# Loads ahead of transposes, weights cast by loads, linear term last: a one-core attention and maxout kernel

## The chip, the cores and the metric

One of the eight cores of a Trainium2 chip runs the whole program. The metric is the device time of one execution in microseconds (us). TensorE multiplies, VectorE and ScalarE move and change data, GpSimd does small sums and issues the loads, SyncE issues the stores and the transposing transfers. The profile calls them PE, DVE, ACT, POOL and SP; PEld is the loading of the weights into TensorE.

## What is computed

```python
B, N, m, C = 4, 12544, 32, 128          # x: (B, N, C), inducing: (m, C)
h = mab(I, x)                           # 32 inducing points attend to the N rows of a batch
y = mab(x, h)                           # every row attends to its batch's 32 rows of h
# mab(q, kv): a = softmax(q @ kv.T / sqrt(C)); return a @ kv
g = max(y @ w1, y @ w2)                 # w1, w2: (128, 1024)
out = g @ w_out                         # w_out: (1024, 128); out: (50176, 128), f32
```

## The kernel before, in words

Since max(p, q) = p + relu(q - p), the output of a row is y @ (w1 @ w_out) + relu(y @ (w2 - w1)) @ w_out, and since y is a mean over the 32 rows of h, two products are made once for each batch: `hwd` = h @ (w2 - w1), 32 x 1024 (`small_hwd`), and `m1` = h @ (w1 @ w_out), 32 x 128 (`small_m1`). For every row TensorE then needs its 32 exponentials `e2` (`stage`), their product with `hwd`, a relu, and the product of that with `w_out`. The denominator `rp` (`dens`) is multiplied in at the very end (`evict_group`).

A batch has 98 chunks of 128 rows. Its tokens come in seven tiles of 14 chunks (`load_x`, a load that casts f32 to f16, issued by GpSimd, L165). Phase one makes h: the tile is transposed into `xT`, `p1_scores` (L239) multiplies it with the inducing points, ScalarE takes the exponential `et` (L248), `p1_accum` (L282) sums et times x. For batch 0 TensorE makes the transposes (`p1_transpose`) and also sums et with a matrix of ones (L269). For batches 1 to 3 the transposes are transfers that SyncE issues, two to a tile (`transpose_x_dma`, L171), the sum of et is made by GpSimd (L290, L295, `small_fold` L300 and L301), and phase one of a batch is spread over the main loop of the batch before it.

The main loop works on blocks of four quarters of the columns. `phase` (L730) makes four matmuls side by side, 32 rows each, whose results four relus of 128 x 512 take out of PSUM, on ScalarE (L746) or VectorE (L749), whichever the planner holds free earlier. `final_one` then makes the eight products with `w_out` for each of four chunks (L575, 32 matmuls of 128 columns), into a PSUM bank that already holds the linear term e2.T @ m1. The first blocks of batch 0 (`full`; the "ramp") are narrow, one or two chunks to a quarter; there the linear term comes from `m1bd`, a block-diagonal copy of m1, by four matmuls ahead of the 32 (L563); in the other blocks it comes from `phase`. `evict_group` scales four chunks (L601, L604, L611) and SyncE stores them (L626), from six buffers.

The order on each engine is written by a planner at build time. Class `Clock` holds an estimate of when each engine and PSUM bank is free, and the main loop picks a phase or a final matmul by it. Side work is tied to a count: `at(n, f, ...)` puts f on a list that `side_work` starts once n chunks of output have been evicted. Since engines work in order, what is written behind a waiting instruction on the same engine waits too.

Weights: three loads (L202 to L204) bring w2, w1 and w_out as f32. `weights_1` subtracts (VectorE, L372). Behind the first two phases and the staging of block 1 stand `weights_2` (a cast of w_out by ScalarE, L376; eight f32 transposes of w1 by TensorE, L383, and two casts of them, L387), `weights_3` (w1 @ w_out, L394, L402) and `small_m1(0)` (L357, L360, and four copies to `m1bd` by ScalarE, L364). Only then come the final matmuls of the first group.

Of the kernel before, what the change touches and what calls it, by code (L numbers as in the profile page):

```python
# [9 lines left out]
F16 = mybir.dt.float16  # L10
# [6 lines left out]
INF = 1e9  # L17
# [91 lines left out]
def kernel(  # L109
# [17 lines left out]
    P1 = 14  # L127
    WARM = 12

# [55 lines left out]
    wof = relup.tile([128, 2, J], F32, name="wof", tag="relu1")  # L185
    woutf = wof[:, 0, :].rearrange("p (jb c) -> p jb c", c=C)
# [7 lines left out]
    with tc.manual_schedule(engines={ET.PE, ET.DVE, ET.Activation, ET.Pool, ET.SP}):  # L194
# [7 lines left out]
        nc.gpsimd.dma_start(out=w2f, in_=moe_w2)  # L202
        nc.gpsimd.dma_start(out=w1f, in_=moe_w1)
        nc.gpsimd.dma_start(out=woutf, in_=moe_w_out.rearrange("(jb j) c -> j jb c", j=128))  # L204
# [47 lines left out]
        def p1_accum(b, i):  # L252
# [3 lines left out]
            if b == 0:  # L256
                last = i == len(parts[0]) - 1
                ck.wait(ready, "p1")
                for j in range(n):
# [6 lines left out]
                    )  # L266
                for j in range(0, n, 4):
# [5 lines left out]
                        start=(i == 0 and j == 0),  # L273
# [80 lines left out]
        def small_m1(b):  # L354
# [6 lines left out]
            if b in (0, 1, 2, 3):  # L361
                for q in range(4):
                    r = slice(32 * q, 32 * (q + 1))
                    nc.scalar.copy(out=m1bds[b % 2][r, q, :], in_=ps[r, 0:128])  # L364
                ck.on_act(end, 0.8)
# [5 lines left out]
        def weights_1():  # L371
            nc.vector.tensor_sub(w21, w2f, w1f)  # L372
            ck.on_dve(0.0, 1.2)

        def weights_2():
            nc.scalar.copy(out=woutp, in_=woutf)  # L376
            ck.on_act(0.0, 1.0)
            for g in range(2):
                bi, ps = bank([128, 512])
                ck.wait(ck.bank[bi], "w")  # L380
                for j in range(4):
                    jb = 4 * g + j
                    nc.tensor.transpose(  # L383
                        ps[:, 128 * j : 128 * (j + 1)], w1f[:, 128 * jb : 128 * (jb + 1)], identity32
                    )
                end = ck.run(0.9)
                nc.scalar.copy(out=w1T[:, 4 * g : 4 * g + 4, :], in_=ps)  # L387
                ck.bank[bi] = w_of["w1T"] = ck.on_act(end, 0.48)

        def weights_3():  # L390
# [12 lines left out]
            ck.bank[bi] = ck.on_dve(end, 0.2)  # L403
# [86 lines left out]


# [61 lines left out]
        def final_one():  # L553
# [4 lines left out]
            if g.ps is None:  # L558
# [3 lines left out]
                for s, (q, t) in enumerate(g.chunks):  # L562
                    nc.tensor.matmul(  # L563
                        out=g.ps[:, 128 * s : 128 * (s + 1)],
                        lhsT=g.blk.e2[:, 128 * t : 128 * (t + 1)],
                        rhs=m1bds[g.blk.quarters[q].b % 2][:, q, :],
                        start=(s == 0),
# [307 lines left out]
```

## Time and profile before

| what | value |
|---|---|
| median of 3 runs | 359.9 us (358.38 to 362.74) |
| the profiled execution, its own time | 362.34 us |
| its span, from the first to the last instruction | 360.6 us |
| mean granted TensorE clock | 0.965 |
| PE, PEld, DVE, ACT, POOL busy | 339.7, 260.9, 291.1, 277.1, 43.2 us |
| DMA | 50.60 MB moved, mean 140 GB/s |

The timeline of slices gives the busy tenths of each engine in 40 equal parts, PEclk being the clock that TensorE was granted in tenths of full speed. In tables by window, each engine has its busy time and, in brackets, its number of instructions; then come the clock, the share of the 16 DMA engines and the rate. In timelines a row has its start, its duration, the engine and line, and in square brackets the idle time before it and what ended that. SPq and POOLq are issues of transfers, not their landing.

### The profile page before, as it was taken

The page shows a single profiled execution, that of the slowest core. Times are in us where ns is not written, and L with a number is a line of the kernel's source. Part 1 is how long each engine was busy: PE and PEld are TensorE (multiplying, and loading weights), DVE is VectorE, ACT ScalarE, POOL GpSimd, SP SyncE. Part 2 cuts the span into 40 slices and gives each one's busy share as a digit, 9 for nine tenths or more (in the row PEclk, how much of TensorE's full clock was granted, in tenths as well). Part 3 has the DMA queues.
Part 4 walks back from the last instruction along what each step waited for, and adds up shares of the span by engine and source line. Part 5 has one row for each costly group of instructions (what it writes and reads, how often), then busy time and mean ns, then how long its engine had stood idle before and what let it go on. Part 6 is the DMA issues. An engine that isn't in the chain of part 4 may idle for free.

```text
span 360.6 us, 13062 instructions
## 1 busy us (share of the span) xinstructions
PE 339.7 (94%) x5655; PEld 260.9 (72%) x5655; DVE 291.1 (81%) x529; ACT 277.1 (77%) x541; POOL 43.2 (12%) x69
## 2 busy tenths in 40 slices
PE   7867989999999994999999998999999999999996
PEld 3754867677778573778777776778777777777786
DVE  1344789998997993799989998688899989999972
ACT  2547789988885893788798987788889888889850
POOL 6320011115000021013200011213000000000000
PEclk9985899999999998899999999899999999999999
DMA  7999559684957799283992699883132223222223
GB/s 134 210 293 214 123 151 146 109 174 105 234 156 162 139 133 204 66 165 115 177 228 91 129 204 146 197 159 116 62 119 88 79 86 121 89 90 89 89 89 133
DMA packets 58089, 50.60 MB, mean 140 GB/s; under 512 B 41104, under 2 KB 41776, under 8 KB 58032
## 3 DMA queue, kind: packets, MB, share of 16 engines
q1 hardware_dynamic: 53424, 35.35, 39.9%
q0 software_dynamic: 4608, 14.42, 21.5%
q8 instruction: 44, 0.72, 0.8%
q14 instruction: 13, 0.11, 0.1%
HBM read 27.28 MB, written 25.69 MB: 147 GB/s over the span
## 4 chain that ended last, share of the span: by engine, by line
PE 78%; DMA 12%; ACT 4%; DVE 3%; issue 1%; POOL 1%; SPq 1%; POOLq 0%; ACTq 0%; DVEq 0%
PE ps L575 50%; PE ps L730 18%; DMA xT<-xn 9%; DMA xn<-in_x_dram 3%; PE ps L435 2%; ACT relu L746 2%; PE ps L239 2%; PE ps L282 2%; DVE relu L749 2%; PE ps L563 1%; PE ps L476 1%; PE ps L320 1%; PE ps L223 0%; ACT xT L230 0%; POOL xn L165 0%
## 5 line engine op out<-in xcount | busy, mean ns | idle before, releaser
L746 ACT ACTIVATE relu<-ps 128x512 f16<-128x512 f32 x449 | 238.5, 601 | 42.0 <-PE ps L730 37.0
L749 DVE TENSOR_SCALAR relu<-ps 128x512 f16<-128x512 f32 x335 | 215.6, 682 | 32.9 <-PE ps L730 28.8
L575 PE MATMUL ps<-woutp,relu 128*128 128x128 f16 x3136 | 226.9, 222 | 0.1
L575 PEld LDWEIGHTS <-relu 128*128 128x128 f16 x3136 | 181.0, 99 | 39.5 <-issue 29.7
L730 PE MATMUL ps<-e,hwd 32*128 32x512 f16 (+2 forms) x928 | 91.6, 359 | 0.4 <-DVE hwd L346 0.4
L601 DVE TENSOR_TENSOR o<-ps,rp 128x512 f32<-128x512 f32 x88 | 60.1, 683 | 9.1 <-PE ps L575 7.0
L730 PEld LDWEIGHTS <-hwd 32*128 32x128 f16 x928 | 25.7, 94 | 23.0 <-issue 2.6
L730 PE MATMUL ps<-m,e 32*128 32x128 f16 x336 | 33.7, 219 | 0.1
L295 POOL TENSOR_TENSOR eacc<-eacc,et 128x448 f32<-128x448 f32 x18 | 18.6, 1035 | 94.0 <-ACT et L248 94.0
L248 ACT ACTIVATE et<-ps 128x448 f16<-128x448 f32 (+2 forms) x29 | 15.6, 539 | 13.0 <-PE ps L239 10.1
L239 PE MATMUL ps<-inducingT,xT 128*128 128x32 f16 x392 | 16.0, 177 | 9.0 <-DMA xT<-xn 8.1
L730 PEld LDWEIGHTS <-e 32*128 32x128 f16 x336 | 19.0, 93 | 2.8 <-issue 0.3
L239 PEld LDWEIGHTS <-xT 128*128 128x128 f16 x392 | 13.3, 96 | 10.4 <-DMA xT<-xn 8.5
L447 ACT ACTIVATE e<-ps 128x512 f16<-128x512 f32 (+2 forms) x31 | 16.4, 529 | 2.3 <-PE ps L435 2.3
L165 POOL DMA_DIRECT2D xn<-in_x_dram x29 | 15.7, 548 | 9.8 <-DMA xn<-in_x_dram 4.9
L227 DVE COPY xT<-ps 128x1024 f16<-128x1024 f16 (+2 forms) x8 | 5.1, 633 | 11.7 <-PE ps L223 11.7
L290 POOL CAST eacc<-et 128x448 f32<-128x448 f16 x3 | 1.7, 558 | 101.0 <-ACT et L248 101.0
L435 PE MATMUL ps<-xT,hT 128*32 128x512 f16 (+2 forms) x124 | 11.4, 359 | 1.3 <-DVE hT L327 1.1
L230 ACT COPY xT<-ps 128x768 f16<-128x768 f16 (+2 forms) x8 | 5.6, 705 | 8.5 <-PE ps L223 8.5
L282 PE MATMUL ps<-et,xn 128*128 128x32 f16 x294 | 10.7, 178 | 0.0
L282 PEld LDWEIGHTS <-xn 128*128 128x128 f16 x294 | 9.9, 97 | 0.1
L223 PE MATMUL ps<-identity,xn 128*128 128x128 f16 x98 | 6.8, 219 | 1.9 <-DMA xn<-in_x_dram 1.9
(61 smaller groups left out, 109.6 us busy)
## 6 DMA issues: line engine op xcount, KB each, us to landing
out_dram<-o SPq DMA_DIRECT2D x96, 256.0 KB, 2.3
xn<-in_x_dram POOLq DMA_DIRECT2D x27, 448.0 KB, 11.8
wf<-in_moe_w_dram POOLq DMA_DIRECT2D x2, 512.0 KB, 14.8
xT<-xn SPq DMA_TRANSPOSE x42, 3.8
wof<-in_moe_w_out_dram POOLq DMA_DIRECT2D x1, 512.0 KB, 14.1
out_dram<-o SPq DMA_DIRECT2D x4, 128.0 KB, 2.4
xn<-in_x_dram POOLq DMA_DIRECT2D x1, 256.0 KB, 13.5
xn<-in_x_dram POOLq DMA_DIRECT2D x1, 192.0 KB, 13.9
```

Of the source, the lines that this page charges most:

```text
L165: nc.gpsimd.dma_start(out=xn_at[b, i][:, 0:n, :], in_=xr[b, :, k0 : k0 + n, :])
L239: nc.tensor.matmul(out=ps[:, j * M : (j + 1) * M], lhsT=xT_tiles[b % 2][:, k0 + j, :], rhs=inducingT, start=True, stop=True,)
L248: nc.scalar.activation(out=et[:, 0:n, :], in_=ps[:, 0 : n * M], func=AF.Exp, scale=scale)
L282: nc.tensor.matmul(out=ps[:, 0:M], lhsT=xn[:, j, :], rhs=et[:, j, :], start=(j == 0), stop=(j == n - 1))
L295: nc.gpsimd.tensor_add(out=acc, in0=acc, in1=et)
L435: nc.tensor.matmul(out=ps[32 * q : 32 * (q + 1), 128 * t : 128 * (t + n)], lhsT=hq, rhs=xT[:, c : c + n, :], start=True, stop=True, tile_p ...
L447: nc.scalar.activation(out=blk.e2[:, 0 : 128 * wd], in_=ps[:, 0 : 128 * wd], func=AF.Exp, scale=scale)
L575: nc.tensor.matmul(out=g.ps[:, 128 * c : 128 * (c + 1)], lhsT=g.blk.relu[q][:, 128 * (jb * w4 + t) : 128 * (jb * w4 + t + 1)], rhs=woutp[: ...
L601: nc.vector.tensor_mul(osb[:, 0:n, :], g.ps[:, 0 : n * C].rearrange("p (s c) -> p s c", s=n), rp)
L730: nc.tensor.matmul(**seq[i])
L746: nc.scalar.activation(out=dst, in_=src, func=AF.Relu)
L749: nc.vector.tensor_scalar(out=dst, in0=src, scalar1=0.0, scalar2=None, op0=ALU.max)
```

## The change

All of it is order, types and places; the mathematics stays.

1. Loads of batches 2 and 3: `load_x(b, i)` at base - 34 + 3 i instead of base - 26 + 6 i, base being the count at which the batch before is done (98, 196). The last is then due at base - 16, before the first transpose and before phase one of that batch. The transposes are due at base - 12 + 3.4 j instead of base - 16 + 4 j.
2. Batch 1: transposes at 9 + 2.3 j instead of 1 + 3 j; scores of tile i at 17 + 5.2 i instead of 10 + 6.3 i.
3. Weights: w2 and w1 come in halves of 512 columns (four loads), w1 comes a second time as f16 (`w1h`), and w_out is cast by its load into `woutp`. `weights_1` subtracts in two halves.
4. `weights_2` has eight f16 transposes of `w1h`, one result copied by VectorE and one by ScalarE, and stands right behind `small_hwd(0)`, ahead of the first phases. `small_m1(0)` becomes side work behind the start of the main loop.
5. In full blocks the four linear matmuls come behind the 32 final ones. The copies to `m1bd` are split between VectorE and ScalarE, in all batches.
6. Batch 0's first five sums of et are made by VectorE, with one f32 matmul of ones at the end; 14 matmuls on the `warm` tile (`fill`) stand between phase one of batch 0 and its first staging.
7. The condition on `tp` near the end is written in another way; with MARGIN = 0 it says the same.

GpSimd at the end of batch 1's phase one, before. The eacc rows are its sums of et for batch 1 (1023) and batch 2 (2982); xn rows are loads of batch 2.

```order
L300 TENSOR_TENSOR eacc_1023<-eacc_1023 128x224
L301 TENSOR_TENSOR eacc_1023<-eacc_1023 128x96
L165 DMA xn_85<-in_x_dram 128x1792
L165 DMA xn_86<-in_x_dram 128x1792
L165 DMA xn_87<-in_x_dram 128x1792
L165 DMA xn_88<-in_x_dram 128x1792
L165 DMA xn_89<-in_x_dram 128x1792
L290 CAST eacc_2982<-et_0_2938 128x448
L165 DMA xn_90<-in_x_dram 128x1792
L165 DMA xn_91<-in_x_dram 128x1792
L295 TENSOR_TENSOR eacc_2982<-eacc_2982,et_1_3118 128x448
```

The same place in the change:

```order
L328 TENSOR_TENSOR eacc_1171<-eacc_1171 128x224
L329 TENSOR_TENSOR eacc_1171<-eacc_1171 128x96
L166 DMA xn_85<-in_x_dram 128x1792
L166 DMA xn_86<-in_x_dram 128x1792
L166 DMA xn_87<-in_x_dram 128x1792
L166 DMA xn_88<-in_x_dram 128x1792
L166 DMA xn_89<-in_x_dram 128x1792
L166 DMA xn_90<-in_x_dram 128x1792
L166 DMA xn_91<-in_x_dram 128x1792
L318 CAST eacc_2984<-et_0_2941 128x448
```

The last two loads have moved ahead of the cast that waits for batch 2's first exponentials. Batch 3 has the same rows with other tiles.

ScalarE in the ramp, before. e rows are exponentials of blocks 1 and 2, relu_568 to 571 belong to block 0.

```order
L349 CAST hwd_561<-ps_565 128x512
L746 ACTIVATE relu_568<-ps_572 128x512
L746 ACTIVATE relu_570<-ps_574 128x512
L746 ACTIVATE relu_568<-ps_596 128x512
L746 ACTIVATE relu_570<-ps_598 128x512
L746 ACTIVATE relu_571<-ps_599 128x512
L447 ACTIVATE e_46_625<-ps_620 128x128
L376 CAST woutp<-wof 128x1024
L387 CAST w1T<-ps_628 128x512
L387 CAST w1T<-ps_634 128x512
L364 CAST m1bd_110<-ps_650 32x128 x4
L447 ACTIVATE e_56_667<-ps_662 128x256
```

And in the change:

```order
L377 CAST hwd_569<-ps_573 128x512
L421 COPY w1T<-ps_582 128x512
L793 ACTIVATE relu_588<-ps_592 128x512
L793 ACTIVATE relu_590<-ps_594 128x512
L793 ACTIVATE relu_588<-ps_616 128x512
L793 ACTIVATE relu_590<-ps_618 128x512
L793 ACTIVATE relu_591<-ps_619 128x512
L481 ACTIVATE e_49_645<-ps_640 128x128
L481 ACTIVATE e_56_666<-ps_661 128x256
L393 CAST m1bd_110<-ps_683 32x128 x2
```

The cast of w_out and one of w1T have left ScalarE, the other w1T copy has moved ahead of the relus, and two copies to m1bd are left, behind the exponentials.

SyncE from its first store on, before: each out row is a group of four chunks, xn_90 and xn_91 are batch 1's first two tiles.

```order
L626 DMA out_dram<-o_758 128x512
L171 DMA_TRANSPOSE xT_95<-xn_90 128x7x128 x2
L626 DMA out_dram<-o_863 128x512
L171 DMA_TRANSPOSE xT_95<-xn_91 128x7x128
L626 DMA out_dram<-o_952 128x512
L171 DMA_TRANSPOSE xT_95<-xn_91 128x7x128
L626 DMA out_dram<-o_1080 128x512
L171 DMA_TRANSPOSE xT_95<-xn_92 128x7x128 x2
```

And in the change:

```order
L672 DMA out_dram<-o_765 128x512
L672 DMA out_dram<-o_836 128x512
L672 DMA out_dram<-o_956 128x512
L172 DMA_TRANSPOSE xT_95<-xn_90 128x7x128 x2
L672 DMA out_dram<-o_1031 128x512
L172 DMA_TRANSPOSE xT_95<-xn_91 128x7x128 x2
L672 DMA out_dram<-o_1111 128x512
L172 DMA_TRANSPOSE xT_95<-xn_92 128x7x128 x2
```

The first transpose stands behind the third group instead of the first, and from there two follow nearly each group.

The diff, cut to its core:

```diff
-    wof = relup.tile([128, 2, J], F32, name="wof", tag="relu1")
-    woutf = wof[:, 0, :].rearrange("p (jb c) -> p jb c", c=C)
+    w1h = relup.tile([128, 4096], F16, name="w1h", tag="relu1")[:, 0:J]
...
-        nc.gpsimd.dma_start(out=w2f, in_=moe_w2)
-        nc.gpsimd.dma_start(out=w1f, in_=moe_w1)
-        nc.gpsimd.dma_start(out=woutf, in_=moe_w_out.rearrange("(jb j) c -> j jb c", j=128))
+        for h in range(2):
+            sl = slice(512 * h, 512 * (h + 1))
+            nc.gpsimd.dma_start(out=w2f[:, sl], in_=moe_w2[:, sl])
+            nc.gpsimd.dma_start(out=w1f[:, sl], in_=moe_w1[:, sl])
+        nc.gpsimd.dma_start(out=w1h, in_=moe_w1)
+        nc.gpsimd.dma_start(out=woutp, in_=moe_w_out.rearrange("(jb j) c -> j jb c", j=128))
...
+                if i < NE:
...
+                        nc.vector.tensor_add(out=acc, in0=acc, in1=et)
...
+                    return
+                if i == NE:
+                    nc.tensor.matmul(out=st[0]["eps"][:, 0:M], lhsT=ones32, rhs=st[0]["ef"],
...
                 for q in range(4):
                     r = slice(32 * q, 32 * (q + 1))
-                    nc.scalar.copy(out=m1bds[b % 2][r, q, :], in_=ps[r, 0:128])
+                    if q % 2:
+                        nc.scalar.copy(out=m1bds[b % 2][r, q, :], in_=ps[r, 0:128])
+                    else:
+                        nc.vector.tensor_copy(out=m1bds[b % 2][r, q, :], in_=ps[r, 0:128])
...
         def weights_1():
-            nc.vector.tensor_sub(w21, w2f, w1f)
+            for h in range(2):
+                sl = slice(512 * h, 512 * (h + 1))
+                nc.vector.tensor_sub(w21[:, sl], w2f[:, sl], w1f[:, sl])
...
         def weights_2():
-            nc.scalar.copy(out=woutp, in_=woutf)
...
-                    nc.tensor.transpose(
-                        ps[:, 128 * j : 128 * (j + 1)], w1f[:, 128 * jb : 128 * (jb + 1)], identity32
-                    )
-                nc.scalar.copy(out=w1T[:, 4 * g : 4 * g + 4, :], in_=ps)
+                    nc.tensor.transpose(ps[:, j, :], w1h[:, 128 * jb : 128 * (jb + 1)], identity16)
+                if g == 0:
+                    nc.vector.tensor_copy(out=w1T[:, 0:4, :], in_=ps)
+                else:
+                    nc.scalar.copy(out=w1T[:, 4:8, :], in_=ps)
...
         small_h(0)
+        fill(14)
         stage(blocks[0])
         weights_1()
         small_hwd(0)
+        weights_2()
...
-                for s, (q, t) in enumerate(g.chunks):
-                    nc.tensor.matmul(out=g.ps[:, 128 * s : 128 * (s + 1)],
...
-                start=False,
-                stop=(jb == NJB - 1),
+                start=(g.blk.full and state["mm"] == 0),
+                stop=(jb == NJB - 1 and not g.blk.full),
...
             if state["mm"] == n * NJB:
+                if g.blk.full:
+                    while "m1" not in st[g.blk.b]:
+                        f, a = pending.pop(0)
+                        f(*a)
+                    for s, (q, t) in enumerate(g.chunks):
+                        nc.tensor.matmul(out=g.ps[:, 128 * s : 128 * (s + 1)],
...
-            p_first, p_step = (10, 6.3) if b == 1 else (2, 7)
-            t_first, t_step = (1, 3) if b == 1 else (-16, 4)
+            p_first, p_step = (17, 5.2) if b == 1 else (2, 7)
+            t_first, t_step = (9, 2.3) if b == 1 else (-12, 3.4)
...
-                    at(base - 26 + 6 * i, load_x, b, i)
+                    at(base - 34 + 3 * i, load_x, b, i)
...
         phase(plan_phase())
         stage(blocks[1])
-        weights_2()
         weights_3()
-        small_m1(0)
+        pending.append((small_m1, (0,)))
```

More of the change, by code (lines that the diff above doesn't have):

```diff
@@ L489, in dens, with fill @@
             ck.bank[bi] = ck.on_dve(end, 0.2)
+        def fill(n):
+            bi, ps = bank([128, 512])
+            for _ in range(n):
+                nc.tensor.matmul(out=ps[:, 0:128], lhsT=warm[:, 0:128], rhs=warm[:, 0:128], start=True, stop=True)
+            ck.run(0.056 * n)
         bi, ps = bank([128, 512])
@@ L792, in side_work @@
                         return
+                    if f is small_m1 and a[0] == 0 and w_of["w1out"] > ck.pe:
+                        return
                     if f in (small_hwd, small_m1) and st[a[0]]["hT4r"] > ck.pe:
```

62 lines of the change are left out of this document (43 added, 19 removed).

## The prediction

> **What bounds the kernel now.** I read the slices first, then a table by stage, then TensorE's waits, then the places where it waits.
>
> ```profile
> PE   7867989999999994999999998999999999999996
> PEclk9985899999999998899999999899999999999999
> DMA  7999559684957799283992699883132223222223
> ```
>
> TensorE is busy in nearly every slice of 9 us. The exceptions are the first five slices, slice 16 (136 to 145 us) and slice 25; in each of them the granted clock dips or has dipped.
>
> ```profile
> 24.00:40.00 16.00, 11.70 (x150) 7.71 (x146) 7.81 (x16) 9.05 (x21) 0.53 (x1) 0.57 0.93 186
> 136.62:141.41 4.79, 0.01 (x2) 0.01 (x1) 0.57 (x1) 0.01 (x1) 0.00 (x0) 0.95 1.10 159
> 141.41:147.60 6.19, 6.19 (x74) 4.68 (x75) 3.72 (x7) 3.73 (x7) 1.03 (x1) 0.50 0.60 169
> 150.00:220.00 70.00, 69.95 (x1197) 54.09 (x1195) 64.94 (x116) 60.75 (x120) 9.49 (x14) 1.00 0.71 150
> 226.37:229.78 3.41, 3.41 (x47) 2.83 (x44) 1.96 (x4) 2.28 (x5) 0.47 (x1) 0.51 0.88 221
> ```
>
> From 150 to 220 us TensorE has no gap (69.95 of 70), VectorE 93% and ScalarE 87%: TensorE sets the pace, and time taken out ahead of such a stretch comes off the end. There are three places to take it from: the ramp (24 to 40 us, 11.7 busy of 16, at a clock of 0.57), a hole of 4.8 us at 137 with 6.2 us at half clock behind it, and a smaller pair at 223.
>
> ```profile
> PE ps L239 <- DMA xT<-xn: 8.1, 4, 4.8
> ```
>
> Scores waiting for a transposed tile: 8.1 us in four waits, one of 4.8. What made it late stands in GpSimd's and SyncE's timelines, in TensorE's, and in the chain of waits (its rows have no engine):
>
> ```profile
> 86.26 2.69 POOL L165 DMA_DIRECT2D xn<-in_x_dram  x5
> 127.52 0.56 POOL L290 CAST eacc<-et 128x448 f32<-128x448 f16 x1 [38.57 <-ACT et L248]
> 128.09 0.54 POOL L165 DMA_DIRECT2D xn<-in_x_dram  x1
> 213.96 1.10 POOL L165 DMA_DIRECT2D xn<-in_x_dram  x2
> ```
> ```profile
> 135.28 5.91 SPq L171 DMA_TRANSPOSE xT<-xn  x1
> ```
> ```profile
> 128.47 12.88 DMA xT<-xn
> 213.77 10.87 DMA xT<-xn
> ```
> ```profile
> 51.99 0.34 PE L239 MATMUL ps<-inducingT,xT 128*128 128x32 f16 x7 [1.18 <-DMA xT<-xn]
> 141.41 0.37 PE L239 MATMUL ps<-inducingT,xT 128*128 128x32 f16 x7 [4.78 <-DMA xT<-xn]
> 224.68 0.34 PE L239 MATMUL ps<-inducingT,xT 128*128 128x32 f16 x7 [1.69 <-DMA xT<-xn]
> ```
> ```profile
> xT<-xn SPq DMA_TRANSPOSE x42, 3.8
> ```
>
> Five loads of batch 2 go out at 86; the last two stand behind a cast that idles 38.57 us for the first exponentials of that batch, so they start at 128, among the transposes. The transpose issued at 128.47 then takes 12.88 us where the median is 3.8, a later issue holds SyncE for 5.91, and TensorE stands. At 214 the same two loads and 10.87 us.
>
> **The change part by part.** *Loads ahead (batches 2 and 3).* All seven loads now stand behind the fold at 85 to 86 us, with no cast between, and nothing they need is late: their buffers were read long before. Seven at some 2.2 us each end 15 us later, before the first transpose is due (88 chunks, past 100 us). What removes the company removes the wait: 4.78 us, and the half clock behind it, in which 6.19 us of TensorE's work took about twice its time, so 3.1. Sum 7.9. For batch 3: 1.69, and half of 3.41, together 3.4. Below: the waits alone, 6.5 for both; above: nothing more. The later start of the transposes costs nothing while each is due 10 chunks before its scores.
>
> *Batch 1.* Two waits are left, 8.1 - 4.78 - 1.69 = 1.6 us, both where a tile's second transpose is issued one group of four chunks before its scores. By the counts one such place stays (tile 3) and the other gets two groups: 0.8, between 0 and 1.6.
>
> *The ramp.* The rows of VectorE, ScalarE and TensorE, one fence each:
>
> ```profile
> 25.13 1.22 DVE L372 TENSOR_TENSOR w<-wf 128x1024 f16<-128x1024 f32 x1
> 27.05 0.69 DVE L346 CAST hwd<-ps 128x512 f16<-128x512 f32 x1 [0.70 <-PE ps L343]
> 28.47 1.88 DVE L749 TENSOR_SCALAR relu<-ps 128x512 f16<-128x512 f32 x3 [0.73 <-PE ps L730]
> 33.76 0.29 DVE L402 CAST w1out<-ps 128x128 f16<-128x128 f32 x1 [3.41 <-PE ps L394]
> 35.28 1.29 DVE L749 TENSOR_SCALAR relu<-ps 128x512 f16<-128x512 f32 x2 [0.58 <-PE ps L730]
> ```
> ```profile
> 28.44 2.56 ACT L746 ACTIVATE relu<-ps 128x512 f16<-128x512 f32 x5 [0.38 <-PE ps L730]
> 30.84 0.32 ACT L447 ACTIVATE e<-ps 128x128 f16<-128x128 f32 x1
> 31.00 1.09 ACT L376 CAST woutp<-wof 128x1024 f16<-128x1024 f32 x1
> 31.93 1.13 ACT L387 CAST w1T<-ps 128x512 f16<-128x512 f32 x2
> 34.79 1.10 ACT L364 CAST m1bd<-ps 32x128 f16<-32x128 f32 x4 [1.72 <-DVE m L360]
> ```
> ```profile
> 16.41 0.95 PE L223 MATMUL ps<-identity,xn 128*128 128x128 f16 x14 [1.31 <-DMA xn<-in_x_dram]
> 29.32 1.97 PE L383 MATMUL ps<-identity,wf 128*128 128x128 f32 x8
> 32.63 1.09 PE L394 MATMUL ps<-woutp,w1T 128*128 128x128 f16 x8 [1.34 <-ACT w1T L387]
> 36.00 2.13 PE L575 MATMUL ps<-woutp,relu 128*128 128x128 f16 x18
> 38.60 0.96 PE L575 MATMUL ps<-woutp,relu 128*128 128x128 f16 x14
> ```
>
> Block 0's eight relus are done at 31.0, yet its final matmuls start at 36.00: between lie the cast of w_out, f32 transposes, w1T, w1out, m1 and m1bd, one after another. Now, step by step: the subtraction ends its halves at 25.75 and 26.35, the first hwd matmul runs under the second half, its cast goes from 26.35 to 27.04 instead of 27.05 to 27.74 (0.7 gained). The f16 transposes, eight by some 0.07 (0.95 for 14), and their copies (half of 1.13 on each of two engines) fall into waits for hwd; phases from about 27.2. ScalarE: hwd to 27.5, w1T to 28.1, five relus (2.56) to 30.6. VectorE: hwd to 27.04, w1T to 27.7, three relus (1.88) to 29.6, w1out to 29.9. TensorE: w1 @ w_out at 28.2 to 28.8, then the final matmuls when all four quarters have a relu, 29.1 instead of 36.00. After ten of them the m1 matmul waits for w1out, to 29.9; the last relu comes at 30.6, the exponential of block 1 (0.32) at 30.95, its phase to 31.3, 13 matmuls, the other phase, the last matmul and the linear term to about 32.7. Before, the last of the first 32 ended at 39.56. That is 6.9 earlier. Not all of it stays: at 39.56 block 1's first four relus were long done (36.57 on VectorE) and its others under way, at 32.7 the first four just end; two relus on each engine, 1.1 to 1.3 us, are to be waited for once. I take 5.8. From below 2, if the clock stays low and a weight comes late; from above 8, if the planner's next phases hide the relus and the first matmuls do not queue.
>
> The clock in that sum is full. Rows of 3.41 us each, the spacing at which the clock changes here:
>
> ```profile
> 14.70:18.11 3.41, 2.02 (x47) 1.84 (x46) 0.69 (x1) 1.28 (x3) 0.53 (x1) 1.00 1.06 203
> 21.53:24.94 3.41, 1.98 (x52) 1.63 (x47) 1.08 (x4) 1.03 (x4) 1.06 (x2) 0.99 1.09 261
> ```
>
> The first (2.02 busy) kept the clock; after the second (1.98) it was halved until 38.5. The 14 matmuls of `fill` add some 0.8 to the second, in a gap where TensorE waits for VectorE anyway, so they cost nothing. The next windows hold about 2.6 by my steps (hwd 0.4, eight transposes 0.6, two phases 0.6, stagings 0.5, w1 @ w_out 0.5), so I expect the clock to hold.
>
> *At no cost.* The sums of et on VectorE lie in phase one, where it idles more than half; five sums by ones come off TensorE, but it waits for x there (1.31 at 16.41) and gets an f32 matmul more. Splitting m1bd moves 0.55 us from ScalarE to VectorE per batch. The linear term behind the finals is the same work. If that cover failed, each would cost under 0.5.
>
> *The weight loads.* The issue of w_out and its landing:
>
> ```profile
> 11.00 0.91 POOL L204 DMA_DIRECT2D wof<-in_moe_w_out_dram  x1 [1.62 <-DMA xn<-in_x_dram]
> ```
> ```profile
> wf<-in_moe_w_dram POOLq DMA_DIRECT2D x2, 512.0 KB, 14.8
> wof<-in_moe_w_out_dram POOLq DMA_DIRECT2D x1, 512.0 KB, 14.1
> ```
>
> w_out landed at 25.1 behind all of x of batch 0. The f16 w1 now has its place, w_out comes one transfer later, some 1.5 us: 26.6. Needed at 26.7 and 28.2: just in time, no cost. Batch 1's loads end 1.5 us later, at about 39.5.
> The Trainium skill ("DMA: Bandwidth & Descriptors", section "Anatomy of one DMA — SWDGE (gpsimd) path") puts a fixed part of about 2.0 us on every transfer that GpSimd issues; three more of them one after another would bring w_out at 31.1 and leave some 3 us less of the ramp, a sum of 15. The trace speaks against paying it in turn: 14 us from issue to landing are a queue in which transfers overlap.
>
> **Sum.** 7.9 + 3.4 + 0.8 + 5.8 = 17.9. The profiled execution took 362.34 us (span 360.6), so its like would take 344.4; that execution lay 2.4 above the median, and the median 359.9 gives **342.0**.
>
> **Rivals.** *The clock falls in the ramp all the same (0.15).* A window with too little work halves it for at least two of 3.41 us, with about 5 us of work in them: 2.5 lost, 344.5. For it: the ramp is full of waits, and the lost window was hardly emptier than the kept one. Against: fill.
> The Trainium skill ("TensorE: Matmul & The Clock Gate", section "Part 4: PE-mode transpose") says that transposes do not count as busy for the clock in the same way, which would take the eight transposes out of the window and give this rival's time. The trace disagrees so far: the kept window had 0.95 of its 2.02 us in transposes, the lost one half as much.
>
> *A weight comes late (0.08).* TensorE works in order, so transposes of w1h placed ahead of the first phases block all of them. Price: each us of lateness past 26.7; with 4 us the ramp gives 1.8, 346.0. Against: the slot at 25.1.
>
> *The transposes are late without the loads (0.12).* Then the reordering does not do what it says: 359.9 - 0.8 - 5.8 = 353.3, no change to a measurement. For it: SyncE's issues bunch. Against: up to 128 us no transpose of batch 2 held anyone.
>
> *Slower (0.03).* Batch 1's transposes, now denser, meet batch 1's own loads, since the ramp is shorter and these loads end later. Two loads in such company cost 7.9, 4.0 each; it outweighs 17.9 from 4.5 loads still under way at the first transpose, and with six the time is 366. Against: the first transpose stands behind the third group, at about 40, when at most one load is left (the DMA slices fall after 38 us).
>
> **How the numbers follow.** The forecast has 0.62 and its own terms' bounds, 339 (20.9 off) to 351.4 (8.5 off). The range takes in the first two rivals and, below, the scatter of runs (358.38 to 362.74 before): 336.5 to 351, leaving out most of the third rival, the fourth and some tail. Faster by over 2% (under 352.7; about what a measurement here can tell from no change): forecast, two rivals and a third of the third, 0.89; within 2%: 0.08; slower: 0.03.
>
> **What would show it.** Right: no wait of a score for xT above 1.5 us, seven loads in one row on GpSimd at about 79 and 156, no clock under 1.00 after 40 us, first final matmul near 29, first store near 33, fold of batch 1 at about 78.5. Wrong: transposes landing in 8 us or more without loads beside them, a wait at the f16 transposes of w1, PEclk at 0.5 between 25 and 38, or new waits of TensorE for relus in the next 20 us that eat the ramp's gain.

## The result, and the profile after

| | us |
|---|---|
| before, median of 4 runs beside the change | 359.28 (358.38 to 362.74) |
| changed, median of 4 runs | 348.85 (348.46 to 349.48) |
| ratio | 0.9694, 95% interval 0.9627 to 0.9761 |
| changed, profiled execution: own time, span, mean clock | 348.85, 346.6, 0.995 |

The change gains 10.4 us. The forecast was 342.0, so its range held and its sum was 6.9 too good. Ratios here and below leave out executions more than 1.5% above the fastest of their kernel, which for the kernel before are many of its longer ones, while the medians are over all.

The timeline of slices of the changed kernel:

```profile
PE   7788998899999999999999999999999999999996
PEclk9989999999999999999999999999999999999999
DMA  7999786763996698674993599851123222222223
```

The holes in slices 16 and 25 are gone, and so is the low clock from 25 to 38 us. What is left of low clock lies in phase one of batch 0 (slice 3). The two 8s in slices 7 and 8 are new: 52 to 69 us, phase one of batch 1. The table by stage (TensorE, weight loads, VectorE, ScalarE, GpSimd, then clock, DMA share and rate) shows the same:

```profile
0.00:24.00 24.00, 19.41 (x303) 14.31 (x304) 9.31 (x23) 10.44 (x16) 12.97 (x30) 0.93 0.98 198
24.00:40.00 16.00, 13.74 (x262) 10.06 (x259) 12.76 (x28) 11.72 (x27) 0.84 (x2) 1.00 1.09 219
40.00:90.00 50.00, 46.63 (x818) 34.83 (x815) 44.98 (x88) 41.49 (x81) 11.57 (x16) 1.00 0.65 143
150.00:220.00 70.00, 69.29 (x1192) 53.65 (x1190) 63.73 (x116) 61.37 (x121) 9.97 (x15) 1.00 0.72 163
```

Before, the first and the third of these stages read

```profile
0.00:24.00 24.00, 18.98 (x335) 14.36 (x335) 6.06 (x17) 10.70 (x17) 11.73 (x27) 1.00 0.95 212
40.00:90.00 50.00, 48.35 (x864) 36.57 (x861) 45.57 (x89) 43.58 (x85) 10.51 (x14) 1.00 0.69 137
```

The ramp, 11.70 busy at a clock of 0.57 before, holds 13.74 at full clock. From 40 to 90 us TensorE idles 3.4 of 50, before 1.7. TensorE's waits for transposed tiles, in us, times, and the longest:

```profile
PE ps L242 <- DMA xT<-xn: 3.1, 3, 1.6
```

It was 8.1 us in four waits. GpSimd's timeline, SyncE's, and the list of issues with the median us to landing at the row's end:

```profile
18.00 0.90 POOL L207 DMA_DIRECT2D woutp<-in_moe_w_out_dram  x1 [0.97 <-DMA xn<-in_x_dram]
83.52 0.66 POOL L328 TENSOR_TENSOR eacc<-eacc 128x224 f32<-128x224 f32 x1
84.74 2.69 POOL L166 DMA_DIRECT2D xn<-in_x_dram  x5
87.64 1.11 POOL L166 DMA_DIRECT2D xn<-in_x_dram  x2 [0.21 <-issue]
123.49 0.56 POOL L318 CAST eacc<-et 128x448 f32<-128x448 f16 x1 [34.74 <-ACT et L251]
160.52 4.02 POOL L166 DMA_DIRECT2D xn<-in_x_dram  x7 [0.17 <-PE ps L510]
```
```profile
35.73 7.57 SPq L672 DMA_DIRECT2D out_dram<-o  x3
43.34 3.40 SPq L172 DMA_TRANSPOSE xT<-xn  x2
46.78 0.58 SPq L672 DMA_DIRECT2D out_dram<-o  x1
47.41 2.61 SPq L172 DMA_TRANSPOSE xT<-xn  x2
```
```profile
xT<-xn SPq DMA_TRANSPOSE x42, 3.2
woutp<-in_moe_w_out_dram POOLq DMA_DIRECT2D x1, 256.0 KB, 7.8
```

All seven loads of a batch go out in a row ahead of the cast, and the median landing of a transpose has gone from 3.8 to 3.2 us. TensorE's timeline shows the ramp and the three waits that are left:

```profile
24.98 0.94 PE L528 MATMUL ps<-warm 128*128 128x128 f16 x14
27.66 0.61 PE L415 MATMUL ps<-identity,w1h 128*128 128x128 f16 x8
30.47 0.72 PE L607 MATMUL ps<-woutp,relu 128*128 128x128 f16 x10
31.02 0.22 PE L385 MATMUL ps<-w1out,hT 128*128 128x128 f16 x1
33.78 0.39 PE L624 MATMUL ps<-m1bd,e 128*128 128x128 f16 x4
48.49 0.34 PE L242 MATMUL ps<-inducingT,xT 128*128 128x32 f16 x7 [0.70 <-DMA xT<-xn]
53.44 0.34 PE L242 MATMUL ps<-inducingT,xT 128*128 128x32 f16 x7 [0.78 <-DMA xT<-xn]
65.54 0.34 PE L242 MATMUL ps<-inducingT,xT 128*128 128x32 f16 x7 [1.63 <-DMA xT<-xn]
```

All three lie in phase one of batch 1; batches 2 and 3 have none. Where the time came from is read by the ends of VectorE's scaling of each group of four chunks, in the two profiled executions (a difference of two ends is the time of that stretch):

| stretch | before | changed | gain | predicted |
|---|---|---|---|---|
| to the end of group 1 (ramp) | 40.68 | 35.70 | 5.0 | 5.8 |
| groups 1 to 28 (phase one of batch 1 and on) | 94.10 | 94.98 | -0.9 | 0.8 |
| groups 28 to 30 (hole of batch 2) | 13.22 | 6.32 | 6.9 | 7.9 |
| groups 30 to 51 | 65.23 | 65.27 | 0.0 | 0 |
| groups 51 to 55 (hole of batch 3) | 17.04 | 14.14 | 2.9 | 3.4 |
| groups 55 to 100 | 127.56 | 127.49 | 0.1 | 0 |
| group 100 to the own time | 4.51 | 4.95 | -0.4 | 0 |
| sum | 362.34 | 348.85 | 13.5 | 17.9 |

Before, the second stretch varies: in four further profiles with the old due times of batch 1 (three of the kernel before, and the loads alone, all below) it took 94.20 to 94.67, so what was lost there is 0.3 to 0.9.

So 4.4 us of the forecast's terms are missing in the profiled pair, and another 3.1 because the profiled execution of before lay that far above the median of 359.28. The theory after this reading: the batch 1 term failed because a tile's second transpose is issued too few groups ahead of its scores, phase one lost something of its own, and the holes of before are not of one size. The rivals: the relus bound the stretch after the ramp and eat the gain whatever the transposes do; the holes are always as large as in the profile.

### The profile page after: what moved, and what is told of

Read it like the earlier page. It is cut to its first block, busy times and chain, and to the rows that moved or that the text cites. A ratio compares the mean times of both kernels' runs of the same rounds, so it can differ in the third digit from the quotient of the medians.

```text
span 346.6 us, 13072 instructions
## 1 busy us (share of the span) xinstructions
PE 332.3 (96%) x5651; PEld 256.0 (74%) x5651; DVE 293.4 (85%) x540; ACT 276.0 (80%) x536; POOL 44.7 (13%) x72
## 4 chain that ended last, share of the span: by engine, by line
PE 81%; DMA 6%; ACT 5%; DVE 3%; SPq 2%; issue 1%; POOL 1%; POOLq 0%; ACTq 0%; DVEq 0%
PE ps L607 52%; PE ps L777 19%; DMA xn<-in_x_dram 3%; ACT relu L793 3%; PE ps L242 2%; PE ps L469 2%; DMA xT<-xn 2%; PE ps L310 2%; DVE relu L796 2%; SPq L172 1%; PE ps L510 1%; PE ps L226 1%; PE ps L348 1%; PE ps L624 1%; ACT xT L233 0%
## 5 line engine op out<-in xcount | busy, mean ns | idle before, releaser
L793 ACT ACTIVATE relu<-ps 128x512 f16<-128x512 f32 x454 | 241.1, 602 | 33.1 <-PE ps L777 28.1
L796 DVE TENSOR_SCALAR relu<-ps 128x512 f16<-128x512 f32 x330 | 212.7, 682 | 21.1 <-PE ps L777 19.4
L607 PE MATMUL ps<-woutp,relu 128*128 128x128 f16 x3136 | 222.3, 220 | 0.4 <-ACT relu L793 0.3
L607 PEld LDWEIGHTS <-relu 128*128 128x128 f16 x3136 | 177.3, 98 | 38.1 <-issue 27.3
L226 PE MATMUL ps<-identity,xn 128*128 128x128 f16 x98 | 7.8, 238 | 1.4 <-DMA xn<-in_x_dram 1.4
```

The source lines that it names most:

```text
L607: nc.tensor.matmul(out=g.ps[:, 128 * c : 128 * (c + 1)], lhsT=g.blk.relu[q][:, 128 * (jb * w4 + t) : 128 * (jb * w4 + t + 1)], rhs=woutp[: ...
L793: nc.scalar.activation(out=dst, in_=src, func=AF.Relu)
L796: nc.vector.tensor_scalar(out=dst, in0=src, scalar1=0.0, scalar2=None, op0=ALU.max)
```

## The experiments

The first four shared the runs of before at 360.44 us (13 runs), the next four those at 359.43 (6 runs), the last four those at 360.88 (13 runs). The change itself was not measured again beside them: each difference from its 348.85 is one across measurements, and its own four executions spread over 1.0 us.

**The loads alone, in the kernel before.**

```diff
-                    at(base - 26 + 6 * i, load_x, b, i)
+                    at(base - 34 + 3 * i, load_x, b, i)
```

> The kernel before with one edit: all seven loads of batches 2 and 3 due before phase one of that batch (base - 34 + 3 i); transposes, ramp and weights as before. If company of two late loads was what held the transposes, no score waits over 1.5 us at batch 2 or 3, no half clock after 40 us, and the time falls by 8 to 11 us, to about 349 to 351. If the transposes are late by themselves, TensorE still waits 2 us or more at 137 and 224 and the time stays within 3 us of 359.

353.17 us (352.23 to 355.33, 4 runs), ratio 0.9865 (0.9752 to 0.9977). The slices and the waits of its profile:

```profile
PEclk9995799999999999999999999999999999999999
```
```profile
PE ps L239 <- DMA xT<-xn: 1.8, 2, 1.1
```

Both holes and the half clock behind them are gone: groups 28 to 30 take 6.26 us, groups 51 to 55 14.09, as in the change. One line of the diff does all that was said of the loads. But the expected 349 to 351 was missed: at the median it brings 7.3 us, by the ratio some 5, not 11.3; in the profiled pair it brings 10.1 (362.34 to 352.23).

**All but items 1 and 2.**

```diff
-            p_first, p_step = (17, 5.2) if b == 1 else (2, 7)
-            t_first, t_step = (9, 2.3) if b == 1 else (-12, 3.4)
+            p_first, p_step = (10, 6.3) if b == 1 else (2, 7)
+            t_first, t_step = (1, 3) if b == 1 else (-16, 4)
...
-                    at(base - 34 + 3 * i, load_x, b, i)
+                    at(base - 26 + 6 * i, load_x, b, i)
```

> The change without its new due times: the loads and transposes of batches 1 to 3 and the scores of batch 1 stand where they stood before; weights, ramp and fill as in the change. If the ramp's gain of 5 us at the first groups carries to the end, 353 to 355 with the old holes at batches 2 and 3 still there. If batch 1's first transposes, now some 5 us earlier, meet batch 1's own loads, the first scores of batch 1 wait over 2 us and the gain is 0 to 2: 357 to 359.

353.99 us, ratio 0.9857 (0.9797 to 0.9916), and its twelve executions fall into two heaps, seven from 351.39 to 354.67 and five from 358.38 to 362.42. The profiled one took 360.77. Its chain of waits and TensorE's timeline:

```profile
37.18 7.18 DMA xT<-xn
126.53 10.01 DMA xT<-xn
208.33 13.11 DMA xT<-xn
```
```profile
43.54 0.34 PE L242 MATMUL ps<-inducingT,xT 128*128 128x32 f16 x7 [2.21 <-DMA xT<-xn]
136.58 0.34 PE L242 MATMUL ps<-inducingT,xT 128*128 128x32 f16 x7 [1.85 <-DMA xT<-xn]
221.49 0.37 PE L242 MATMUL ps<-inducingT,xT 128*128 128x32 f16 x7 [3.97 <-DMA xT<-xn]
```

Two things follow. The ramp gains without the loads: its first group ends at 35.21. And with batch 1's old due times its first two transposes, issued at 35.66 and 37.18, take 7.84 and 7.18 us: the last three of batch 1's own loads land at 36.98, 39.40 and 42.56, so this is the place of the rival that ended slower. The third to the fourth group take 8.30 us there, against 2.57 in the change. The median is as expected for a gain that carries to the end, the wait of 2.21 us in the profiled execution is as expected for the other case. Why seven of twelve executions are cheap stays open, since a cheap one has no profile.

**Batch 1's due times back, all else kept.**

```diff
-            p_first, p_step = (17, 5.2) if b == 1 else (2, 7)
-            t_first, t_step = (9, 2.3) if b == 1 else (-12, 3.4)
+            p_first, p_step = (10, 6.3) if b == 1 else (2, 7)
+            t_first, t_step = (1, 3) if b == 1 else (-12, 3.4)
```

> The change with batch 1 back at its old due times (transposes 1 + 3 j, scores 10 + 6.3 i), all else as in the change. If the new due times themselves cost the 2.6 us that are lost between groups 3 and 18, about 346. If they keep the transposes off batch 1's own loads, which run to 40 us, then with the first transposes at 36 us the first scores wait 2 us or more, perhaps with a half clock behind, and the time is 349 to 354.

350.32 us (349.79 to 350.75, 4 runs), ratio 0.9776 (0.9677 to 0.9875): 1.5 above the change. Its table by window (columns as above):

```profile
42.00:45.00 3.00, 1.57 (x26) 1.03 (x27) 0.52 (x2) 0.82 (x2) 0.22 (x1) 0.78 1.23 277
45.00:48.00 3.00, 3.00 (x53) 2.16 (x50) 2.27 (x5) 1.88 (x4) 0.34 (x1) 0.66 0.55 149
```

The hole and the half clock after the third group are there, and its fourth group ends at 50.17 instead of 45.51. Yet its tenth ends at 73.68 and the change's at 73.77: most of what the change's later transposes save at 43 us it pays back by 73 us (0.7 of it is phase one, which let this run's first group end at 35.03 instead of 35.70). Item 2 trades one wait for another, and 1.5 us are left of it at the end.

**No fill.**

```diff
-        fill(14)
```

> The change without the 14 matmuls on the warm tile ahead of the first staging. If these keep the clock, it falls to 0.50 for at least 3.4 us between 25 and 38 us, the first store comes 1 to 2.5 us later, and the time is 350 to 351.5. If the rest of the ramp is dense enough by itself, the clock stays at 1.00 there and the time is within 0.5 us of the change's 348.9.

349.74 us (349.62 to 349.94, 4 runs), ratio 0.9761 (0.9664 to 0.9857). Slices and windows of its profile:

```profile
PEclk9986999999999999999999999999999999999999
```
```profile
24.74:28.16 3.42, 1.75 (x33) 0.98 (x32) 3.16 (x7) 0.92 (x3) 0.22 (x1) 1.00 1.08 214
28.16:34.99 6.83, 6.63 (x93) 5.13 (x89) 4.42 (x11) 4.94 (x12) 0.00 (x0) 0.50 1.07 212
```

Without the 14 matmuls the window in the ramp holds 1.75 us, and the next 6.83 us run at half clock. In the change the stretch from 25.0 to 28.4 holds 2.50 at full clock. The first group ends 1.6 us later, the last 1.1: `fill` is worth 0.9 at the median. The clock fell as expected; the time stayed 0.3 under the expected 350 to 351.5.

**Later scores in batch 1.**

```diff
-            p_first, p_step = (17, 5.2) if b == 1 else (2, 7)
+            p_first, p_step = (25, 4.6) if b == 1 else (2, 7)
```

> The change with one number pair altered: the scores of batch 1's tile i are due at 25 + 4.6 i chunks instead of 17 + 5.2 i. The transposes stay where they are. A tile's second transpose is then issued three to four groups of four chunks before its scores, instead of two (tile 3: one). Theory (the distance is too short for transposes that are issued in pairs): the three waits of a score for xT, 3.1 us in all, go, and batch 1's phase one stops giving back ramp gain: 346.0 to 347.0 against the change's 348.85, and the 22nd group ends 2 to 3 us earlier than the change's 110.8. Rival (the relus bound the stretch from 40 to 75 us, the waits only use time that the relus would have cost): the waits go too, but new waits of TensorE for relus take their place, the 22nd group ends within 0.7 us of 110.8 and the time is 348.2 to 349.2.

346.35 us (345.87 to 348.07, 4 runs), ratio 0.9652 (0.9584 to 0.9720). TensorE has no wait for xT left in its list; its longest row for relus and the stage from 40 to 90 us are

```profile
PE ps L777 <- ACT relu L793: 1.7, 3, 0.7
```
```profile
40.00:90.00 50.00, 49.54 (x866) 36.97 (x862) 47.59 (x91) 44.42 (x87) 11.57 (x16) 1.00 0.75 152
```

3.1 us of waits for xT are gone and 0.5 of waits for relus have come (1.2 in the change), the 22nd group ends at 107.73 instead of 110.80, and the time is 2.5 lower. Of the 3.1 us at the 22nd group 0.6 stand at the first already; groups 1 to 28 take 92.81 instead of 94.98, so the waits were worth 2.2. The distance theory holds and the relu rival falls: VectorE was at 90% in that stage and takes 95% without holding TensorE up.

**All sums of et by TensorE again.**

```diff
-    NE = 5
+    NE = 0
```

> The change with NE = 0: all seven sums of et of batch 0 are made by TensorE with the matrix of ones again, and VectorE's five sums and the f32 matmul are gone. Theory (without these matmuls one window of phase one falls short of what keeps the clock, and the half clock that follows costs about 1 us): no granted clock below 1.00 before 24 us, phase one ends about 1 us earlier, first store at 34.7 instead of 35.7, time 347.9. Rival (phase one is paced by the arrival of x, the clock there costs nothing): the first store stays within 0.3 us of 35.7 and the time at 348.85 within 0.4. Second rival (the f32 matmuls of ones were worth taking off TensorE): 349.3 or more.

347.62 us (347.03 to 347.83, 4 runs), ratio 0.9673 (0.9613 to 0.9734): 1.2 below the change. The stage of phase one, and SyncE's first stores:

```profile
0.00:24.00 24.00, 20.47 (x343) 14.97 (x344) 6.27 (x18) 10.69 (x17) 12.76 (x29) 1.00 0.98 198
```
```profile
34.33 7.57 SPq L672 DMA_DIRECT2D out_dram<-o  x3
```

No half clock before 24 us, and the first store 1.4 earlier than the change's 35.73. In the change the window ahead of the half clock reads

```profile
13.03:16.44 3.41, 1.80 (x42) 1.51 (x40) 1.22 (x2) 1.71 (x3) 0.43 (x1) 1.00 1.08 214
```

1.80 us, in which TensorE waits for x and the sums by ones are missing. Of the seven profiled executions with NE = 5 six have a half clock in phase one (the run with the linear term first has not), of the seven with all sums on TensorE none before 24 us. So taking the sums by ones away mostly costs the clock there; how the window is judged is not shown.

What that half clock costs is a part of the 1.2 only. The time of an execution is 2.1 to 2.3 us longer than its span in every execution with NE = 5, and 1.7 to 1.9 in every one with all sums on TensorE, those of the kernel before included: 0.4 us lie outside the span, where no row shows them. And in this profile TensorE waits 0.4 us for x in phase one, in the change's 1.4, which can account for most of the 1.4 at the first store. The spans alone differ by 0.8 at the median (345.9 and 346.6); how that divides between the clock and the arrival of x stays open.

**The linear term first again, weights and loads as in the change.**

```diff
+                for s, (q, t) in enumerate(g.chunks):
+                    nc.tensor.matmul(out=g.ps[:, 128 * s : 128 * (s + 1)],
...
-        pending.append((small_m1, (0,)))
+        small_m1(0)
```

> The change with one part undone: in full blocks the four linear matmuls stand ahead of the 32 final ones again, and small_m1(0) stands right behind weights_3, as in the kernel before; the weights, the loads and all due times stay as in the change. Theory (the order lets the finals start before m1 is ready, and m1 comes about 2.5 us behind the first relus): the first final matmul moves from 30.5 to about 33, the first group ends 1.5 to 2.5 us later than 35.7, and since TensorE sets the pace all of it reaches the end: 350.4 to 351.4. Rival (the relus of blocks 0 and 1 bound the ramp, and finals that start earlier only wait for them): the first group is later, but by 55 us the two have met, and the time is 348.5 to 349.4.

351.71 us (350.70 to 352.52, 4 runs), ratio 0.9784 (0.9730 to 0.9838): 2.9 above the change. TensorE's timeline and two windows:

```profile
23.85 0.94 PE L528 MATMUL ps<-warm 128*128 128x128 f16 x14
30.47 1.12 PE L605 MATMUL ps<-m1bd,e 128*128 128x128 f16 x4 [0.24 <-DVE m1bd L395]
31.43 0.66 PE L617 MATMUL ps<-woutp,relu 128*128 128x128 f16 x9
```
```profile
28.88:32.30 3.42, 2.41 (x40) 1.46 (x37) 1.68 (x6) 2.44 (x7) 0.00 (x0) 1.00 1.06 211
32.30:35.70 3.40, 3.40 (x55) 2.96 (x44) 2.46 (x4) 2.17 (x4) 0.00 (x0) 0.50 1.08 214
```

Its first final matmul comes at 31.43, 7.6 us behind the start of the fill; in the change it is 5.5. So the order is worth 2.1 us there, and in this execution a window at half clock followed besides. The end moves by about as much: 1.9 us in the two profiles, though phase one ended 1.1 earlier here, and 2.9 at the median. So nothing of the ramp's gain is seen to be lost to the relus of blocks 0 and 1. The upper end of what had been expected, 351.4, was passed by 0.3.

**Both improvements together.** The edits of the later scores and of NE = 0.

> The two edits together: scores of batch 1's tile i at 25 + 4.6 i, and all sums of et of batch 0 on TensorE. If both theories hold, their gains lie in different stretches and add up: 2.3 and 1.0 off the change's 348.85, 345.5. If the relus bound the stretch from 40 to 75 us, both are lost there: 348.2 to 349.2. If only the later scores help, 346.5; if only the ones, 347.9.

345.75 us (345.21 to 345.91, 4 runs), ratio 0.9617 (0.9567 to 0.9666), the fastest of all: 3.1 below the change, where the two apart make 2.5 and 1.2. In its profile TensorE waits 2.3 us for x in phase one (0.4 with NE = 0 alone, 1.4 in the change), and its first group ends at 35.52, hardly before the change's 35.70: without half clock there, the arrival of x can take back what the clock gave. Against the later scores alone NE = 0 brings 0.6, of which 0.4 lie outside the span.

**The loads late, inside the change.**

```diff
-                    at(base - 34 + 3 * i, load_x, b, i)
+                    at(base - 26 + 6 * i, load_x, b, i)
```

> The change with the loads of batches 2 and 3 back at base - 26 + 6 i, all else kept (the transposes at base - 12 + 3.4 j, and batch 1's new due times too). Theory (two late loads among the transposes make the holes, of a size that changes from execution to execution): the times spread over 5 us or more, between 351 and 359, with a median of about 353, so that the loads are worth some 4 us inside the change and not 11.3. Rival (the holes are as large in each execution as in the profiled one): 358 to 360 with a spread under 3 us. Second rival (the later and denser transposes are what matters, the loads nothing): 348.85 within 1.

360.16 us (359.22 to 362.08, 10 runs), ratio 0.9998 (0.9960 to 1.0036). The expectation that I favoured fell, and its first rival held: inside the change the loads are worth 11.3 us (348.85 to 360.16), with a spread of 2.9 over ten executions. The reason is in the chain and in TensorE's timeline:

```profile
128.18 8.70 DMA xT<-xn
212.65 9.49 DMA xT<-xn
```
```profile
136.16 0.34 PE L242 MATMUL ps<-inducingT,xT 128*128 128x32 f16 x7 [2.38 <-DMA xT<-xn]
222.19 0.34 PE L242 MATMUL ps<-inducingT,xT 128*128 128x32 f16 x7 [4.08 <-DMA xT<-xn]
```

A landing of 9.49 us costs a wait of 4.08 here; in the kernel before one of 10.87 at that place cost 1.69. The change issues the transposes later, so the time in hand has shrunk from 9.2 us (10.87 - 1.69) to 5.4. So the 11.3 are not the loads' worth in the kernel before: with loads and transposes both at their old places, and batch 1's old due times, the median was 353.99. The two halves of item 1 belong together. Beside late loads the later transposes are a loss; with early loads, where a transpose lands in 3.2 us, they cost nothing that shows.

**The kernel before, three more profiled executions.**

> The kernel before, unaltered, in another execution with a profile. Theory (the size of the holes varies): TensorE's wait of scores for xT is not 8.1 us in it but anything from 3 to 9, the half clock behind the hole at 136 is shorter or missing where that wait is short, and the time follows them: about 351 plus the waits plus half of the time at half clock behind them. Rival (the holes are alike and the scatter of the times comes from the ramp): 8.1 us of waits within 0.5, one of them 4.8, whatever the time.

> A third profiled execution of the kernel before. The theories expect what they expect of the second: waits of scores for xT anywhere from 3 to 9 us and a time that follows them, or 8.1 us each time.

> A fourth profiled execution of the kernel before, as the two ahead of it: waits of scores for xT anywhere from 3 to 9 us and a time that follows them, or 8.1 us each time.

The holes as groups 28 to 30 over the 6.3 us and groups 51 to 55 over the 14.1 us that they take without one:

| execution | own time | landing of the transpose issued at 128 | wait for it | both holes | time less holes |
|---|---|---|---|---|---|
| the first | 362.34 | 12.88 | 4.78 | 9.9 | 352.5 |
| again 2 | 357.31 | 12.33 | 4.22 | 5.5 | 351.8 |
| again 1 | 356.01 | 11.03 | 2.93 | 4.4 | 351.6 |
| again 3 | 354.00 | 9.80 | 1.70 | 2.4 | 351.6 |

The rows of the last, chain and timeline:

```profile
128.24 9.80 DMA xT<-xn
```
```profile
138.09 0.34 PE L239 MATMUL ps<-inducingT,xT 128*128 128x32 f16 x7 [1.70 <-DMA xT<-xn]
```

The program is the same, the transpose is issued at 128 in each, and its landing varies by 3 us. The wait is the landing less 8.1 us, and a wait of 2.93 or more brings one or two windows of half clock with it. The landing in turn follows the second of the two loads: that landed at 140.51, 140.39, 138.12 and 137.77 (in the order of the table), and the transpose 0.8, 0.3, 0.9 and 0.3 us later. Less its holes the kernel takes 351.6 to 352.5 each time, near where the loads alone ended (353.17). The theory that the holes vary holds.

The table also prices the half clock. What a hole takes beyond its wait is 2.1 us where the clock was halved for 6.83 us (the first, at 141), and 1.3 where it was halved for 3.41 (the first at 226, again 1 and again 2 at 141); without half clock it is 0.1 (again 3 at 138).

## Why the prediction was right or wrong

**What bounds the kernel, and the cause of the holes: right.** The two loads behind the cast were the company that made the transposes late. Putting them early removed the holes and their half clock, alone (353.17) and inside the change (11.3 us, with the later transposes kept). The seven loads took longer than said, 22.9 us from the first issue at 84.74 instead of 15, but the last still landed at 107.6, ahead of the first transpose at 111.

**Loads, 7.9 and 3.4: the mechanism right, the size of the wrong execution.** In the profiled pair they gave 6.9 and 2.9. The other 1.5 is the price of the half clock: I took half of the work done in it, 3.1 and 1.7, and the holes of that execution took 2.1 and 1.3 beyond their waits. The larger error is a step of the sum. I wrote "its like would take 344.4; that execution lay 2.4 above the median, and the median 359.9 gives 342.0", and so took the holes of that execution off a median whose holes are smaller. The three further profiles show holes of 2.4 to 5.5 where that one had 9.9, and the loads alone bring 7.3 at the median. By the last table what that execution lay above the others was hole, so on these terms the forecast should have stayed at 344.4: the change leaves no such hole, and its runs lie within about 1.0 us.

**"The later start of the transposes costs nothing": right only with the early loads.** With late loads the wait in batch 3 is 4.08, where the four profiles of the kernel before have 1.69 at most.

**Batch 1, 0.8 gained: failed, -0.9.** I counted that a distance of two groups would cure one of the two places. Three places waited, 3.1 us. The longest wait, 1.63, is at tile 3, the place that was said to stay at a distance of one group. The other two had two groups and waited 0.70 and 0.78: SyncE now sends two transposes one behind the other (3.40 us of issuing at 43.34), and a distance of two groups from the second of a pair to its scores does not cover issue and landing; three to four do (346.35). The mark that I had set, no such wait above 1.5 us, was missed by one of 1.63, and the fold of batch 1 came at 83.52 instead of 78.5. The move of the transposes out of the way of batch 1's own loads was worth something, since with the old due times a hole of some 5 us stands at 43; but with the scores this close most of it was paid back within 30 us, and 1.5 us stayed.

**The ramp, 5.8: 5.0, and right but for phase one.** From the end of phase one on it went as worked out: no wait at the transposes of w1, first final matmul at 30.47 where 29.1 was said, 1.0 of the difference being phase one's own delay (its last sums end at 25.05, before at 24.08). With all sums of et on TensorE the first final matmul came at 29.07. The 1.1 us taken off for the relus are in the sum; that nothing more was lost to them fits the linear term's 2.9 us at the end.

**The sums of et "at no cost": failed, 1.2.** I looked for cover on VectorE and found it; what the sums by ones had also done was to keep the clock. In phase one they filled windows that are short of work while x arrives. I had used the kept window of 2.02 us to argue for `fill`, and did not apply it to the five sums taken out of those windows. But the clock is at most 0.8 of the 1.2: the 0.4 us that the change loses behind the last group come with NE = 5 in every execution and lie outside the span, and their cause is open. The price that I had named should the cover fail was under 0.5.

**The clock in the ramp: held, as expected.** Without `fill` it falls (349.74). The comparison behind it was weaker than it looked: cut at the edge where the clock changed, 24.88, the lost window of before holds 2.04 us, as much as the kept one with 2.02. And a lost window does not cost "at least two" at half clock, as the rival had it: the one at 226 in the kernel before cost one, as the one at 16.4 in the change did.
The Trainium skill ("TensorE: Matmul & The Clock Gate", "Part 1: The HAM clock gate") describes a free-running window of about 3.4 us. The trace agrees: in all 14 profiles each stretch at half clock inside the work was 3.41 us or a whole multiple of it, up to 13.65.

**The weights: in time.** The transposes of w1 at 27.66 have no wait before them; w_out, issued at 18.00, landed 7.8 us later, at 25.8, where 26.6 was forecast.
The Trainium skill ("DMA: Bandwidth & Descriptors", "Anatomy of one DMA — SWDGE (gpsimd) path") has a fixed part of some 2.0 us for each such transfer. Three more of them did not cost it in turn here, which would have brought w_out at 31.1.

**The rivals.** The clock in the ramp and the late weight did not happen; the transposes land in 3.2 us without company, so the third fell too. The slower one had its place right, at the third group, and its price far too high: in the run with the old due times it costs 1.5 us. The change escapes it by its later due times, as argued, though both ends had moved: batch 1's last load landed at 41.6 and not 39.5, and the first transpose was issued at 43.34 and not at 40.

In numbers: 342.0 and 2.4 for the median step is 344.4; 0.8 for the ramp (phase one), 1.7 for batch 1, 1.5 for the price of the half clock and 0.4 outside the span make 348.8. The time lies inside the forecast's own bounds too, 339 to 351.4, and that is in part luck: they held neither the median step nor a loss in batch 1, and gave the sums of et under 0.5. The slack that had been left for other terms covered these.

## What to carry to other kernels

A stall that is read from one profiled execution is a draw. Take it off that execution's own time, or profile the old kernel two or three times before pricing its removal: the same program gave holes of 9.9, 5.5, 4.4 and 2.4 us. Moving the consumer of a transfer is as much a part of a reorder as moving the transfer: count the distance from issue to use in us behind the last transfer of a pair. And before small work is taken off TensorE in a stretch that waits for data, look whether that work is what keeps the clock, and compare times as well as spans.

## What the runs showed of the hardware

- A transposing transfer issued at the same place of the same program landed in 9.80, 11.03, 12.33 and 12.88 us beside two loads, each time within 0.9 us behind the landing of the second of them, and in 2.92 us (issued at 128.92) where only the loads had been moved.
- Cut at the edges where the clock changes, the 14 profiles have 21 windows of 3.41 us at full clock with 0 to 2.00 us of TensorE's work inside the program, and half clock followed each of them. Between 2.0 and 2.4 us both happened: windows of 2.04, 2.05, 2.20, 2.25 and 2.41 lost the clock, windows of 2.02, 2.09 and 2.10 kept it. Busy time alone does not settle which window loses it.
- In the kernel before, a stretch of 3.41 us at half clock behind a hole cost 1.3 us of time in each of three cases, one of 6.83 cost 2.1: less than half of the stretch.
- With batch 1's old due times the fourth group ended 4.7 us behind the change's, the tenth 0.1 ahead of it: by then the change had had three waits of its own. A hole is worth what the end shows.
